# Half-block units of a mixture-of-experts kernel: tokens stationary, weights moving, in the first layer

## The chip, the cores and the metric

The kernel runs on one core of a Trainium2 chip. The metric is the device time of one execution in microseconds (us). Engines are named TensorE (PE in the profile; PEld are its weight loads), VectorE (DVE), ScalarE (ACT), GpSimd (POOL) and SyncE (SP, which issues most of the transfers).

## What is computed

A pooled attention makes 4608 rows of 512 numbers, and a mixture of eight experts is applied to them, each row going through the one expert that its gate picks:

```python
logits = x @ w_gate                      # x: 4608 x 512, the attention's output
expert_idx = np.argmax(logits, axis=1)
...
gate_w = probs[np.arange(N), expert_idx]
for e in range(E):                       # E = 8
    mask = expert_idx == e
    ...
    xe = x[mask]
    h = np.maximum(xe @ w1[e], 0.0)      # w1[e]: 512 x 1024
    ye = h @ w2[e]                       # w2[e]: 1024 x 512
    out[mask] = gate_w[mask, None] * ye
```

With the inputs that are timed here the experts get 1018, 55, 333, 239, 827, 724, 24 and 1388 rows.

## The kernel before

The first part (attention, gate, scattering the rows by expert) is not touched. The second part, in the function `experts`, works in **units**: up to 512 rows of one expert, counted in half blocks of 64 rows (n = 1 to 8). Here there are 13 units, numbered from 0, and their n is 8, 8, 1, 6, 4, 8, 5, 8, 4, 1, 8, 8, 6. The change concerns the units with n = 1, which are unit 2 (55 rows of expert 1) and unit 9 (24 rows of expert 6). The plan of the units is a table that every engine reads into registers, so each engine's program has branches by n.

Full precision is kept by splitting: every operand is a high part, rounded to the matmul's format, and a low part, the rest. W1H, W1L, W2H, W2L are the parts of an expert's two weight matrices in SBUF, XH and XL those of the rows (transposed, features by rows), HH and HL those of the hidden layer. For n = 1 the low parts of the 64 rows stand beside the high ones in 128 columns.

For a unit, the engines do this:

- TensorE (`form`): the first layer `mm1`, in eight slices of 128 hidden features (`f` = 0 to 7; L860 is its matmul, weights stationary, rows moving). A slice goes to one of three PSUM banks, pP0, pP1 and pq, in turn, so slice f waits until the low part of slice f - 3 is done (`V_h`), and it waits for the two parts of its piece of weights (`split`). Then, for n up to 2, the next unit's rows are transposed (`xt_all`, L813), and the second layer follows (`product`, L882), for n = 1 with 16 matmuls of 512 columns, two for each k of eight. The second layer's piece for k = 6 and 7 is the last that it waits for.
- ScalarE: for each slice the Relu that makes the high part (`hhi`, L968), and between them the casts of the unit's four second-layer pieces (`whi` 4 to 7, L1058); then the next unit's rows (`xhi`, L1031) and the casts of the next unit's four first-layer pieces (`whi` 0 to 3), all in program order.
- VectorE: for n up to 2 first the sum of the two halves of a slice in PSUM (`hsum`, L973), then the low part of the hidden slice (`hlo`, L989), and one low part of weights (`wlo`, L1066, piece 4). Then the next unit's rows (`xlo`, L1046), its pieces 0 and 2 (`wlo`), and the unit's own output (`y`, which for a half block is three operations, L1165, L1167 and L1169, by way of Y2), and then the next unit's slices.
- GpSimd: the previous unit's scatters of output rows (L1357), the low parts of pieces 5, 6 and 7 (L1066), then of the next unit's pieces 1 and 3.
- SyncE: in one queue the rows of a later unit (L1245), their gates (L1237), and the pieces of a later expert's weights into the staging tile ST (L1280). The second-layer pieces wait, where n is under 3, until the unit's second layer is done:

```python
                    if half:
                        with sp.If(entry(sp, K_U, u, 1, 8) < 3):
                            sp.wait_ge(Q["P_y"], 4 * u + 4)
                    for i in ii:
                        free(i)
                        stage_piece(i, e)
```

A wait of any engine holds what stands behind it in that engine's program. What the sums read and write before:

```python
dve.tensor_reduce(out=H1[g % 3], in_=pH[g % 3][:, : 2 * P].rearrange("p (a t) -> p t a", a=2), ...)   # PSUM to PSUM
src = H1[g % 3] if n <= 2 else pH[g % 3]
return dve.scalar_tensor_tensor(out=dst[:, f, to], in0=src[:, at], scalar=0.0, in1=f32(HH[:, f, at]), ...)
```

## Time and profile before

| | us |
|---|---|
| median of 3 runs | 624.31 (624.09 to 625.96) |
| profiled execution, its own time | 623.57 |
| its span in the profile | 621.9 |
| unit 2 on TensorE (its first matmul to unit 3's) | 263.47 to 277.19 |
| unit 9 on TensorE (its first matmul to unit 10's) | 476.67 to 491.33 |

The times in the profile count from the span's start. A row of a timeline has start, duration, engine, line, operation, what it writes from what it reads, shape and count, and in brackets the idle time ahead of it with what ended it. Rows of groups have the busy time and the mean duration of one in ns after the bar. In the chain of work that ended last, each row is a stretch of the path that sets the end.

### The profile page before, as it was taken

The numbers are of one execution on the slowest core, as the hardware profiler recorded it, in microseconds if no ns is written. First come the engines' busy times: TensorE is split into PE (matmuls) and PEld (weight loads), VectorE is DVE, ScalarE is ACT, GpSimd is POOL, SyncE is SP. The second block draws the span as 40 slices with busy tenths as digits, with TensorE's granted clock in tenths as the row PEclk, the third lists the DMA queues.
The fourth block names the chain that finished last, engine by engine and source line by source line (L and its number), as shares of the span: only waits on it lengthen the run. The fifth ranks groups of instructions, "written<-read, shape, count | busy, mean of one in ns | idle before, by whom it ended". The sixth has DMA issues, their size and how long they took to land.

```text
span 621.9 us, 13480 instructions
## 1 busy us (share of the span) xinstructions
PE 598.6 (96%) x4412; PEld 510.8 (82%) x4412; DVE 349.7 (56%) x731; ACT 240.5 (39%) x453; POOL 243.3 (39%) x288
## 2 busy tenths in 40 slices
PE   6989999999999999999999999999999999999995
PEld 5778989888877888899897889888898878888994
DVE  7699898888761325377576433854146764133220
ACT  2567776876511114075364311523034541021110
POOL 7457656655321222278545311251106861101101
PEclk9999999999999999999999999999999999999999
DMA  8999997981334671719578551074305360101001
GB/s 321 368 277 280 301 286 250 250 252 61 130 119 137 175 244 47 220 40 307 181 213 270 137 173 36 3 213 137 104 35 159 84 188 23 53 0 37 36 4 53
DMA packets 93937, 96.47 MB, mean 155 GB/s; under 512 B 43102, under 2 KB 74846, under 8 KB 93792
## 3 DMA queue, kind: packets, MB, share of 16 engines
q1 hardware_dynamic: 85808, 74.27, 41.0%
q0 software_dynamic: 7440, 20.50, 9.0%
q8 instruction: 60, 0.98, 0.6%
q14 instruction: 85, 0.70, 0.4%
q10 hardware_dynamic: 544, 0.02, 0.0%
HBM read 72.68 MB, written 26.00 MB: 159 GB/s over the span
## 4 chain that ended last, share of the span: by engine, by line
PE 72%; DVE 9%; issue 5%; POOL 4%; SPq 3%; ACT 3%; DMA 2%; POOLq 1%; DVEq 0%; ACTq 0%
PE pU L882 31%; PE pP L860 18%; PE pq L860 9%; PE pU L299 4%; DMA XE<-in_v_dram 2%; PE pP L283 2%; PE pP L463 2%; POOL dispatched L407 2%; PE pS L263 2%; SPq L1245 1%; PE pq L253 1%; ACT W L1058 1%; DVE mx L267 1%; DVE raw L172 1%; POOL raw L172 1%
## 5 line engine op out<-in xcount | busy, mean ns | idle before, releaser
L882 PE MATMUL pU<-W,H 128*128 128x512 f32 x912 | 216.4, 397 | 0.0
L882 PEld LDWEIGHTS pU<-W,H 128*128 128x128 f32 x912 | 171.3, 188 | 41.0
L860 PE MATMUL pP<-X,W 128*128 128x512 f32 (+3 forms) x748 | 143.2, 345 | 2.9 <-DVEq L1406 1.6
L860 PEld LDWEIGHTS pP<-X,W 128*128 128x128 f32 x748 | 122.8, 188 | 19.6 <-DVE H L989 2.3
L1357 POOL DMA_INDIRECT out_dram<-Y,GT x51 | 54.2, 1063 | 192.5 <-DVE Y L1171 169.4
L1066 POOL TENSOR_TENSOR W<-ST,W 128x1024 fp32r<-128x1024 f32 x30 | 77.7, 2605 | 84.1 <-ACT W L1058 84.0
L968 ACT ACTIVATE H<-pP 128x512 fp32r<-128x512 f32 (+1 forms) x67 | 36.0, 537 | 189.0 <-PE pP L860 153.2
L1171 DVE TENSOR_SCALAR Y<-pU,GT 128x512 f32<-128x512 f32 x36 | 27.0, 750 | 106.6 <-PE pU L882 105.6
L989 DVE SCALAR_TENSOR_TENSOR H<-pP,H 128x512 fp32r<-128x512 f32 (+2 forms) x73 | 42.2, 580 | 69.8 <-ACT H L968 68.0
L860 PE MATMUL pq<-X,W 128*128 128x512 f32 (+3 forms) x364 | 72.9, 348 | 0.9 <-DVE H L989 0.6
L860 PEld LDWEIGHTS pq<-X,W 128*128 128x128 f32 x364 | 60.1, 188 | 9.9 <-DVE H L989 1.1
L1058 ACT CAST W<-ST 128x1024 fp32r<-128x1024 f32 x56 | 57.1, 1056 | 7.6 <-DMA ST<-in_moe_w_dram 7.6
L299 PE MATMUL pU<-V,pt 110*128 110x146 f32 (+3 forms) x468 | 56.7, 283 | 1.3 <-ACT pt L284 0.8
L299 PEld LDWEIGHTS pU<-V,pt 110*128 110x128 f32 (+3 forms) x468 | 51.4, 179 | 3.0 <-ACT pt L284 1.8
L1066 DVE TENSOR_TENSOR W<-ST,W 128x1024 fp32r<-128x1024 f32 x26 | 42.7, 1645 | 7.5 <-ACT W L1058 7.4
L407 POOL DMA_INDIRECT dispatched<-xe,ix x36 | 39.8, 1107 | 18.2 <-POOL ix L368 9.8
L968 ACT ACTIVATE H<-pq 128x512 fp32r<-128x512 f32 (+1 forms) x33 | 17.9, 541 | 70.6 <-PE pq L860 69.1
L989 DVE SCALAR_TENSOR_TENSOR H<-pq,H 128x512 fp32r<-128x512 f32 (+2 forms) x35 | 20.8, 594 | 28.3 <-ACT H L968 27.5
L284 ACT COPY pt<-pP 110x384 f32<-110x384 f32 x72 | 30.9, 481 | 6.5 <-PE pP L283 5.8
L276 ACT ACTIVATE P<-sd 128x576 f32<-128x576 f32 x36 | 24.8, 689 | 19.6 <-DVE sd L270 17.7
L172 POOL TENSOR_TENSOR raw<-raw 128x768 f32<-128x768 f32 (+1 forms) x18 | 26.6, 1476 | 13.0 <-DMA raw<-in_v_dram 12.2
L1046 DVE TENSOR_TENSOR X<-pS,X 128x512 fp32r<-128x512 f32 x34 | 22.0, 687 | 16.9 <-ACT X L1031 11.3
(185 smaller groups left out, 624.6 us busy)
## 6 DMA issues: line engine op xcount, KB each, us to landing
ST<-in_moe_w_dram SPq DMA_DIRECT2D x56, 512.0 KB, 6.1
raw<-in_k_dram SPq DMA_DIRECT2D x12, 768.0 KB, 7.2
raw<-in_v_dram SPq DMA_DIRECT2D x11, 768.0 KB, 9.1
XE<-dispatched SPq DMA_DIRECT2D x104, 64.0 KB, 2.3
qa<-in_q_dram SPq DMA_DIRECT2D x24, 256.0 KB, 7.3
w<-in_moe_w_dram SPq DMA_DIRECT2D x8, 512.0 KB, 4.7
XE<-dispatched SPq DMA_DIRECT2D x15, 256.0 KB, 3.4
qa<-in_q_dram SPq DMA_DIRECT2D x2, 1024.0 KB, 11.3
```

The costliest lines, as they stand in the source:

```text
L172: return lambda: eng.tensor_tensor(out=out, in0=raw[:, :, 0:n], in1=raw[:, :, n : 2 * n], op=ALU.add)
L284: take(out=pt[t][a][0:R], in_=pPs[a][0:R, 0 : 3 * P])
L299: nc.tensor.matmul(pu[p0 : p0 + n, a, h * VW : (h + m) * VW], lhsT=pt[t][a][0:r, c % 3 * P + p0 : c % 3 * P + p0 + n], rhs=Vs[g % 2][0:r, ...
L407: apart(nc.gpsimd.indirect_dma_start(out=xs, out_offset=bass.IndirectOffsetOnAxis(ap=at, axis=0), in_=rows, in_offset=None))
L860: r = pe.matmul(out=pH[g % 3][:, :m], lhsT=w1s(w, f, k), rhs=x, start=i == 0, stop=i == len(passes) - 1)
L882: r = pe.matmul(out=pY[:, s % 2, :], lhsT=h, rhs=w[:, k * 512 : (k + 1) * 512], start=start and i == 0, stop=stop and i == len(ps) - 1, sk ...
L968: act.activation(out=HH[:, f, o], in_=src[:, o], func=AF.Relu).then_inc(Q["A_h"], 1)
L989: return dve.scalar_tensor_tensor(out=dst[:, f, to], in0=src[:, at], scalar=0.0, in1=f32(HH[:, f, at]), op0=ALU.max, op1=ALU.subtract)
L1058: act.copy(out=(W1H if i < 4 else W2H)[:, o], in_=ST[:, i, :]).then_inc(Q["A_s1" if i < 4 else "A_s2"], 1)
L1066: eng.tensor_tensor(out=(W1L if i < 4 else W2L)[:, o], in0=ST[:, i, :], in1=f32((W1H if i < 4 else W2H)[:, o]), op=ALU.subtract).then_inc( ...
L1171: r = dve.tensor_scalar(out=Y[:, s, :], in0=a, scalar1=gate, scalar2=None, op0=ALU.mult)
L1357: pool.indirect_dma_start(out=out, out_offset=bass.IndirectOffsetOnAxis(ap=GT[:, u, s, 1:2].bitcast(I32), axis=0), in_=Y[:, s, :], in_offs ...
```

## The change

For n = 1 the first layer is turned around. The 128 columns of the rows (64 high, 64 low) are the stationary operand, and the weights move, 512 columns at a time: two halves of the hidden layer (a = 0, 1), each with four blocks k of input features and two weight parts, 16 matmuls. The result has rows by partition, so ScalarE copies a half (128x512) to SBUF (`htake`, tile HR), TensorE transposes it in four pieces into another bank (`ht`), and VectorE adds the high rows' part and the low rows' part (`hsums`, tile HS, in SBUF). The Relu (`hhi1`) and the low part (`hlo1`) then work on 128x256, a half of the hidden layer, in place of eight slices of 128x64. The low parts of the rows are put beside the high ones in XH (`xnone`). The second half's transposes stand between the transposes of the next unit's rows, its Relu and low part behind the first block of the next unit's rows. Other units are as they are.

```diff
+    HR = sb.tile([P, 2, 512], F32, name="HR")
+    HS = sb.tile([P, 2, 256], F32, name="HS")
...
-        def xt_all(u):
+        def xt_all(u, mid=lambda: None):
             xt01(u)
+            mid()
...
+        halves_of = lambda w: w.rearrange("p (a i k f) -> p a k i f", a=2, i=2, k=4)
+        rows_h = [HR[:, a, :] for a in range(2)]
+        sums_h = [HS[:, a].rearrange("p (f t) -> p f t", f=4) for a in range(2)]
+        def hbank(u, a):
+            return pH[(8 * u + a) % 3]
+        def tbank(u, a):
+            return pH[(8 * u + (2, 0)[a]) % 3]
+        def mm1_rows(u, a, ks=range(4)):
+            if ks[0] == 0:
+                pe.wait_ge(Q["V_h"], 8 * u - 2 + a)
+                for i in range(2):
+                    split(pe, "s1", u, 2 * a + i)
+            for k in ks:
+                for w in (W1H, W1L):
+                    r = pe.matmul(out=hbank(u, a).rearrange("p (i f) -> p i f", i=2), lhsT=XH[:, k, 0:P], rhs=halves_of(w)[:, a, k],
+                                  start=k == 0 and w is W1H, stop=k == 3 and w is W1L, skip_group_check=True)
+            if ks[-1] == 3:
+                r.then_inc(Q["P_h"], 2)
+        def ht(u, a):
+            if a == 0:
+                pe.wait_ge(Q["V_h"], 8 * u)
+            pe.wait_ge(Q["A_h"], 8 * u + 2 + 2 * a)
+            for f in range(4):
+                r = pe.transpose(tbank(u, a)[:, f * P : (f + 1) * P], rows_h[a][:, f * P : (f + 1) * P], ident)
+            r.then_inc(Q["P_h"], 2)
...
-                mm1(u, n)
+                if n > 1:
+                    mm1(u, n)
+                else:
+                    mm1_rows(u, 0)
+                    mm1_rows(u, 1, range(2))
+                    ht(u, 0)
+                    mm1_rows(u, 1, range(2, 4))
...
-                more(pe, u + 1, lambda: xt_all(u + 1) if u else xt01(u + 1))
+                turned = (lambda: ht(u, 1)) if n == 1 and u > 0 else (lambda: None)
+                more(pe, u + 1, lambda: xt_all(u + 1, turned) if u else xt01(u + 1), turned)
...
+        def htake(u, a):
+            act.wait_ge(Q["P_h"], 8 * u + 2 + 4 * a)
+            act.copy(out=rows_h[a], in_=hbank(u, a)).then_inc(Q["A_h"], 2)
+        def hsums(u, a):
+            dve.wait_ge(Q["P_h"], 8 * u + 4 + 4 * a)
+            dve.tensor_reduce(out=sums_h[a], in_=tbank(u, a).rearrange("p (f a t) -> p f t a", f=4, a=2), axis=AX.X, op=ALU.add).then_inc(Q["V_1"], 4)
+        def hhi1(u, a):
+            act.wait_ge(Q["V_1"], 8 * u + 4 + 4 * a)
+            act.activation(out=HH[:, 4 * a : 4 * a + 4, 0:64], in_=sums_h[a], func=AF.Relu).then_inc(Q["A_h"], 2)
+        def hlo1(u, a):
+            dve.wait_ge(Q["A_h"], 8 * u + 6 + 2 * a)
+            dve.scalar_tensor_tensor(out=HH[:, 4 * a : 4 * a + 4, 64:128], in0=sums_h[a], scalar=0.0, in1=f32(HH[:, 4 * a : 4 * a + 4, 0:64]),
+                                     op0=ALU.max, op1=ALU.subtract).then_inc(Q["V_h"], 4)
...
+        def xnone(u, v):
+            if v < 2:
+                return vnop("V_x", v)
+            with dve.If(entry(dve, K_U, u, 1, 8) < 2):
+                dve.drain()
+                dve.tensor_tensor(out=XH[:, :, 64:P], in0=xbank(0, False).rearrange("p (k t) -> p k t", k=4)[:, :, 0:64], in1=f32(XH[:, :, 0:64]), op=ALU.subtract).then_inc(Q["V_x"], v)
...
-                    go(1)
+                    with act.If(entry(act, K_SW, u, 0, 1) == 1):
+                        whi(u, 4)
+                        whi(u, 5)
+                        htake(u, 0)
+                        whi(u, 6)
+                        whi(u, 7)
...
+                    htake(u, 1)
+                    hhi1(u, 0)
...
-                    go(1)
+                    with dve.If(entry(dve, K_SW, u, 0, 1) == 1):
+                        wlo(u, 4)
...
+                    hsums(u, 0)
+                    hlo1(u, 0)
+                    hsums(u, 1)
...
-        def xpart(eng, u, f, nop, mid=lambda: None, turn=None):
+        def xpart(eng, u, f, nop, mid=lambda: None, turn=None, first=lambda: None):
             f(u, 0, 1)
+            first()
             f(u, 1, 1)
...
+                        go(True, first=lambda: hhi1(u, 1))
...
+                        go(small=True, first=lambda: hlo1(u, 1))
```

The first `go(1)` is in ScalarE's `hidden_hi`, the second in VectorE's `hidden_lo`; `xpart` splits the next unit's rows on both.

The order on the engines shows it at the places that the prediction speaks of, all in unit 2's branch for n = 1. First TensorE, before (the last two of eight slices, then the next unit's rows; XE holds those, pS, pm and pU are PSUM):

```order
L860 MATMUL pP_66<-X,W 128x256 x8
L860 MATMUL pq<-X,W 128x256 x8
L813 MATMUL pS<-ident,XE_3050 128x128 x8
L839 COMPARE_AND_BRANCH
L840 COMPARE_AND_BRANCH
L813 MATMUL pm<-ident,XE_3050 128x128 x4
```

And TensorE in the changed program, from the unit's start:

```order
L885 MATMUL pP_66<-W,X 128x512 x8
L885 MATMUL pq<-W,X 128x512 x4
L896 MATMUL pP_65<-ident,HR 128x128 x4
L885 MATMUL pq<-W,X 128x512 x4
L815 MATMUL pS<-ident,XE_3050 128x128 x8
L896 MATMUL pP_66<-ident,HR 128x128 x4
L842 COMPARE_AND_BRANCH
L843 COMPARE_AND_BRANCH
L815 MATMUL pm<-ident,XE_3050 128x128 x4
```

Eight slices of eight matmuls have become sixteen matmuls, with the first half's transposes among the second half's products and the second half's behind two blocks of the next unit's rows.

VectorE before, at the end of the unit (sum of one slice, low parts, then the next unit's rows):

```order
L973 TENSOR_REDUCE pq<-pq 128x128
L989 SCALAR_TENSOR_TENSOR H<-pP_66,H 128x64
L989 SCALAR_TENSOR_TENSOR H<-pq,H 128x64
L1115 UNCONDITIONAL_BRANCH
L1179 COMPARE_AND_BRANCH
L1121 COMPARE_AND_BRANCH
L1046 TENSOR_TENSOR X<-pS,X 128x4x128 x2
```

And VectorE in the changed program, the unit's hidden layer:

```order
L1137 TENSOR_TENSOR W<-ST,W 128x1024
L1197 UNCONDITIONAL_BRANCH
L796 COPY scr<-scr 128x1
L1199 UNCONDITIONAL_BRANCH
L1013 TENSOR_REDUCE HS<-pP_65 128x256
L1021 SCALAR_TENSOR_TENSOR H<-HS,H 128x4x64
L1013 TENSOR_REDUCE HS<-pP_66 128x256
```

The sixteen small operations are four, of which two read HS and H in place of a PSUM bank; the second low part follows the first block of the next unit's rows:

```order
L1107 TENSOR_TENSOR X<-pS,X 128x4x128
L1021 SCALAR_TENSOR_TENSOR H<-HS,H 128x4x64
L1107 TENSOR_TENSOR X<-pS,X 128x4x128
L1081 COMPARE_AND_BRANCH
L1107 TENSOR_TENSOR X<-pm,X 128x4x128
```

Here the low part has moved in between the next unit's first and second block.

More of the change, by code (lines that the diff above doesn't have):

```diff
@@ L1046, in xlo @@
             dve.tensor_tensor(out=XL[:, :, o], in0=xbank(s, spare).rearrange("p (k t) -> p k t", k=4), in1=f32(XH[:, :, o]), op=ALU.subtract).then_inc(Q["V_x"], inc)
+        def xnone(u, v):
[4 more added lines that the diff above has]
+                dve.tensor_tensor(out=XH[:, :, 64:P], in0=xbank(0, False).rearrange("p (k t) -> p k t", k=4)[:, :, 0:64], in1=f32(XH[:, :, 0:64]), op=ALU.subtract).then_inc(Q["V_x"], v)
+            with dve.Else():
+                vnop("V_x", v)
         def split(eng, n, u, i):
@@ L1092, in hidden_hi @@
                 with act.Else():
-                    go(1)
+                    with act.If(entry(act, K_SW, u, 0, 1) == 1):
[4 more added lines that the diff above has]
+                        whi(u, 7)
+                    with act.Else():
+                        anop("A_s2", 4)
+                        htake(u, 0)
+                    htake(u, 1)
+                    hhi1(u, 0)
         def hidden_lo(u, fs=range(8), small=True):
@@ L1115, in hidden_lo, with next_part @@
                 with dve.Else():
-                    go(1)
-        def next_part(eng, u, xf, xnop, wf, wnop, turn=None, mid=lambda: None, between=2):
+                    with dve.If(entry(dve, K_SW, u, 0, 1) == 1):
+                        wlo(u, 4)
+                    with dve.Else():
+                        vnop("V_s2", 2)
+                    hsums(u, 0)
+                    hlo1(u, 0)
+                    hsums(u, 1)
+        def next_part(eng, u, xf, xnop, wf, wnop, turn=None, mid=lambda: None, between=2, first=lambda: None):
             sw = entry(eng, K_SW, u, 0, 1)
             with eng.If(sw == 0):
-                xpart(eng, u, xf, xnop, mid, turn)
+                xpart(eng, u, xf, xnop, mid, turn, first)
                 wnop()
@@ L1125, in next_part @@
                 ii = range(4) if eng is act else (0, 2)
-                xpart(eng, u, xf, xnop, lambda: [mid(), *(wf(u, i) for i in ii if i < between)], turn)
+                xpart(eng, u, xf, xnop, lambda: [mid(), *(wf(u, i) for i in ii if i < between)], turn, first)
                 for i in ii:
@@ L1139, in following, with go @@
             def following():
-                def go(small):
-                    next_part(act, u + 1, lambda *a: xhi(*a, small), lambda v: anop("A_x", v), whi, lambda: anop("A_s1", 4), between=0 if small else 2)
+                def go(small, **first):
+                    next_part(act, u + 1, lambda *a: xhi(*a, small), lambda v: anop("A_x", v), whi, lambda: anop("A_s1", 4), between=0 if small else 2, **first)
                 if u == 0:
@@ L1147, in following, with alone @@
                 with act.Else():
-                    go(True)
+                    with act.If(entry(act, K_U, u, 1, 8) > 1):
+                        go(True)
+                    with act.Else():
+                        go(True, first=lambda: hhi1(u, 1))
+            def alone():
+                if u > 0:
+                    with act.If(entry(act, K_U, u, 1, 8) < 2):
+                        hhi1(u, 1)
             if u > 0:
                 hidden_hi(u)
-            more(act, u + 1, following)
+            more(act, u + 1, following, alone)
             if u + 2 < NU:
@@ L1174, in following @@
             def following():
-                go = lambda turn=None, small=False, **mid: next_part(dve, u + 1, lambda *a: xlo(*a, small), lambda v: vnop("V_x", v), wlo, lambda: vnop("V_s1", 2), turn,
+                go = lambda turn=None, small=False, **mid: next_part(dve, u + 1, lambda *a: xlo(*a, small), lambda v: xnone(u + 1, v), wlo, lambda: vnop("V_s1", 2), turn,
                                                                      between=0 if small else 2, **mid)
@@ L1181, in following, with alone @@
                 with dve.Else():
-                    go(small=True)
+                    with dve.If(n > 1):
+                        go(small=True)
+                    with dve.Else():
+                        go(small=True, first=lambda: hlo1(u, 1))
                     early()
+            def alone():
+                if u > 0:
+                    with dve.If(n < 2):
+                        hlo1(u, 1)
+                early()
             def early():
@@ L1205, in dve_unit @@
                 hidden_lo(u)
-            more(dve, u + 1, following, early)
+            more(dve, u + 1, following, alone)
             if u + 2 < NU:
```

## The prediction

> **What bounds the kernel now.** I read the page's busy shares first, then TensorE's timeline, then the chain of work that ended last around the units that the change touches, then the timelines of VectorE, GpSimd, ScalarE and the DMA queue there.
>
> ```profile
> PE 598.6 (96%) x4412; PEld 510.8 (82%) x4412; DVE 349.7 (56%) x731; ACT 240.5 (39%) x453; POOL 243.3 (39%) x288
> ```
>
> TensorE is busy for 96% of the span, so time on it counts, unless it then stands waiting. Which units have one half block is read from the widths of L860's matmuls and the counts of L882's. Two units have 64 matmuls of 256 columns (8 a slice) and then 16 of L882: unit 2, from 263.47, and unit 9, from 476.67 (counted from 0). Unit 2 on TensorE (start, duration, engine, line, count):
>
> ```profile
> 240.97 22.65 PE L882 MATMUL pU<-W,H 128*128 128x512 f32 x96
> 263.47 1.12 PE L860 MATMUL pP<-X,W 128*128 128x256 f32 x8
> 264.43 1.12 PE L860 MATMUL pq<-X,W 128*128 128x256 f32 x8
> ...
> 272.01 1.14 PE L813 MATMUL pS<-ident,XE 128*128 128x128 f32 x8
> ...
> 273.38 3.98 PE L882 MATMUL pU<-W,H 128*128 128x512 f32 x16
> 277.19 4.40 PE L860 MATMUL pP<-X,W 128*128 128x384 f32 x24
> ```
>
> A matmul of 512 columns takes 0.234 us there (96 from 240.97 to 263.47), one of 256 columns 0.12 us (8 in 0.96). Unit 3 begins at 277.19, and its fourth slice stands still until VectorE is ready, as the chain shows:
>
> ```profile
> 280.59 0.69 DVE Y L1165
> ...
> 283.70 0.61 DVE H L989
> 284.31 0.04 issue
> 284.36 4.50 PE pP L860 x24
> ```
>
> So what counts at the first place is not when TensorE ends unit 2, but when VectorE has done unit 2's output (three operations from 280.59) and unit 3's first slice. VectorE in turn waits here for GpSimd:
>
> ```profile
> 264.63 0.43 DVE L973 TENSOR_REDUCE pP<-pP 128x128 f32<-128x256 f32 x1 [0.21 <-PE pP L860]
> 265.21 0.98 POOL L1357 DMA_INDIRECT out_dram<-Y,GT  x1 [4.65 <-DVE Y L1171]
> 267.44 7.14 POOL L1066 TENSOR_TENSOR W<-ST,W 128x1024 fp32r<-128x1024 f32 x3 [1.25 <-ACT W L1058]
> 269.67 0.22 DVE L989 SCALAR_TENSOR_TENSOR H<-pP,H 128x64 fp32r<-128x64 f32 x1
> 273.64 1.29 DVE L1046 TENSOR_TENSOR X<-pS,X 128x512 fp32r<-128x512 f32 x2 [0.49 <-ACT X L1031]
> 275.66 1.23 DVE L1066 TENSOR_TENSOR W<-ST,W 128x1024 fp32r<-128x1024 f32 x1
> 276.65 5.88 POOL L1066 TENSOR_TENSOR W<-ST,W 128x1024 fp32r<-128x1024 f32 x2 [2.06 <-ACT W L1058]
> 277.55 2.70 DVE L1066 TENSOR_TENSOR W<-ST,W 128x1024 fp32r<-128x1024 f32 x1 [0.67 <-ACT W L1058]
> 281.38 1.44 DVE L1167 TENSOR_SCALAR Y<-Y,GT 64x512 f32<-64x512 f32 x1
> 401.29 0.48 DVE L1167 TENSOR_SCALAR Y<-Y,GT 64x512 f32<-64x512 f32 x1
> ```
>
> GpSimd's split of a piece takes 7.14 / 3 = 2.38 us. VectorE's takes 1.23 alone (275.66) and 2.70 beside GpSimd (277.55). Taken as a queue for one door this fits: GpSimd's first split ends at 276.65 + 2.39 = 279.04, VectorE's then needs 1.21, which is 280.25, its recorded end; GpSimd's second ends at 282.53, some 2.3 later. VectorE's scaling of Y2 behaves alike (1.44 beside GpSimd, done 0.29 after its end at 282.53; 0.48 without). But VectorE operations with an input in PSUM, in the middle of GpSimd's three splits (269.67, 273.64), take what they always take. So: **a VectorE operation that reads only SBUF waits for the GpSimd split that is running, and the next split waits for it; one that reads PSUM does not.**
>
> **The change, part by part.** Removed on TensorE, a unit: 64 x 0.12 = 7.68 us. Added: 16 x 0.234 = 3.75 for the turned products, and 8 transposes at 0.121 (8 of L813 from 272.01 to 272.98) = 0.97. Net 2.96 us less work a unit, 5.9 in all. What lies behind it decides how much of that is left.
>
> The new steps' durations, from the nearest rows:
>
> ```profile
> L255 ACT COPY qT<-pq 128x512 f32<-128x512 f32 x36 | 21.2, 589 | 11.5 <-PE pq L253 11.3
> L968 ACT ACTIVATE H<-pq 128x512 fp32r<-128x512 f32 x28 | 16.8, 599 | 69.1 <-PE pq L860 69.1
> 272.67 0.22 ACT L968 ACTIVATE H<-pq 128x64 fp32r<-128x64 f32 x1 [0.74 <-DVE pq L973]
> 273.02 1.07 ACT L1031 CAST X<-pS 128x512 fp32r<-128x512 f32 x2
> 274.55 3.91 ACT L1058 CAST W<-ST 128x1024 fp32r<-128x1024 f32 x4
> L267 DVE TENSOR_REDUCE mx<-pS 128x8 f32<-128x576 f32 x36 | 27.1, 752 | 4.4 <-PE pS L263 4.4
> L989 DVE SCALAR_TENSOR_TENSOR H<-pq,H 128x512 fp32r<-128x512 f32 x28 | 19.3, 688 | 27.6 <-ACT H L968 27.3
> ```
>
> The copy of a half out of PSUM is L255's form, 0.59 (0.5 apart in a row of them). The Relu of 256 columns lies between 0.22 (64) and 0.60 (512): 0.38. The sum over 512 elements lies between 0.43 (256) and 0.75 (576): 0.70. The low part of 256 columns lies between 0.22 and 0.69 by width: 0.42; but both its inputs, HS and HH, are now in SBUF, where before one was PSUM. No row shows this operation beside a split. Its lower bound is 0.42 (it passes, as L989 does), its upper 0.42 plus what is left of a split, up to 2.38 (it queues, as L1066 and L1167 do). I take the upper: both operations seen that read SBUF alone queue, and what set L989 apart, its PSUM input, is gone.
>
> *Unit 2, on the profile's clock.* ScalarE may start when TensorE ends unit 1 (240.97 + 22.65 = 263.62): four casts at 0.955, two copies between them at 0.5, the first Relu 0.38, ends 263.66 + 3.82 + 1.0 + 0.38 = 268.86. TensorE keeps ahead of the copies (products done at 267.9). GpSimd is free after its scatter at 266.19 and its casts are there, so its splits run 266.19, 268.57, 270.95. The first low part asks at 268.9, 0.3 us after the second split began, and waits until 270.95: done 271.4. The third split moves to 271.4-273.75. Behind the low part on VectorE stands the sum of the second half (0.70, done 272.05); its Relu is done at 272.45, and the second low part waits for the third split: 273.75-274.2. L882's first eight matmuls run meanwhile, from 271.4; the last eight end near 276.1, against 277.36 now: TensorE is 1.3 us early.
>
> Behind that stands the next unit. ScalarE's second X cast starts at 272.45 instead of 273.5 (the second of the two from 273.02), so GpSimd's first split for unit 3, which now comes 3.15 after that, could start at 275.6. VectorE's second X operation starts after the low part, at 274.15; now 1.4 lie from there (274.26) to its split at 275.66, so it asks at 275.5. VectorE comes first by 0.1 (up to 0.2, since each handover in the rows overlaps by about 0.1). Then split, GpSimd's split, split, and unit 2's output follow as now, 0.1 to 0.5 us earlier. The fourth slice starts so much earlier than 284.36: **0.3 us gained, of 2.96**. Before VectorE's sums and Relus went slice by slice under the matmuls; now the last of them are bare, but those waits are inside this sum. ScalarE's copies (4 x 0.5 in both units) replace small Relus and lie inside it too.
>
> The transfers of unit 3's second-layer pieces wait for the end of unit 2 on TensorE, so they come 1.3 early, no limit. What xnone adds (one VectorE operation, 128x256 from PSUM, under 0.69, in units 1 and 8) is hidden by L882 there (22.65 us in unit 1; 48 matmuls, 11 us by 0.234 each, in unit 8): without that cover 0.4 each.
>
> *Unit 9.* Here GpSimd first issues four scatters, then splits, and TensorE's gain is spent in unit 10 (first the timelines of GpSimd, the DMA queue and TensorE, then the chain):
>
> ```profile
> 481.65 7.17 POOL L1066 TENSOR_TENSOR W<-ST,W 128x1024 fp32r<-128x1024 f32 x3
> 480.01 10.14 SPq L1245 DMA_DIRECT2D XE<-dispatched  x16
> 490.78 2.78 SPq L1237 DMA_DIRECT2D GT<-dispatched  x4
> 491.33 3.03 PE L860 MATMUL pq<-X,W 128*128 128x512 f32 x12 [0.23 <-issue]
> 496.17 3.70 DMA ST<-in_moe_w_dram
> 499.89 1.06 ACT W L1058
> 500.97 1.23 DVE W L1066
> 502.20 0.61 DVE H L989
> 502.86 5.86 PE pP L860 x24
> ```
>
> The splits start at 481.65 whatever TensorE does. Reckoned as above, the low parts go between them at 484.0 and 486.8, the third ends near 489.5, and unit 10 starts near 490.5 instead of 491.33. But its fifth slice (502.86) waits for a chain that starts with a transfer at 496.17. SyncE issues that one after the x rows (until 490.15) and gates (until 493.56) in a row. Its wait for the end of unit 9 (273.38 + 3.98 is the like in unit 2; here about 491) is over by then, so TensorE's being early doesn't move it. So 0.8 are early and 0.8 are waited: **0**.
>
> **Sum:** -0.3 + 0 = -0.3 us. The profiled execution took 623.57 (span 621.9 and 1.67 around it), so 623.3; the median of the runs is 624.31, 0.74 above, and 0.3 off that is **624.0 us**. A change under about 0.3% (1.9 us) can't be told from none.
>
> [...]
>
> **The rivals.**
>
> *The low parts pass.* If this operation is like L989 as it was, they take 0.42 each. The second sum ends at 270.15, the X casts and ScalarE's casts for unit 3 run 2.6 us earlier than 274.55, and with them VectorE's output and the fourth slice: -2.6, so 621.7. For it: no row shows the new form beside a split. Against it: two forms that queue. 0.22.
>
> *The first low part slips in.* If it asks before 268.57 (0.3 earlier than I reckon), or GpSimd starts 0.3 later, one split's wait is saved, and unit 3's fourth slice moves by 1.9: 622.4. 0.07.
>
> *GpSimd takes the door first (the other side).* At the start of unit 3 both ask within 0.1 us. If VectorE's ask comes more than 0.1 later than reckoned, GpSimd's split runs first, VectorE's first split ends at 279.2 instead of 276.9, its second at about 282.5, and the output and the fourth slice slip 1.0 to 1.5: 625.5. For it: today's margin of 0.99 (275.66 against 276.65) is used up. Against it: the handovers' overlap. 0.20.
>
> *All of TensorE's saving counts*, 5.9: 618.4. Against it stand both waits above. 0.02.
>
> **How the numbers follow.** The forecast has 0.44 and its own range is 623.5 to 624.6; 0.05 is for what I don't see. The range reaches from the first rival with a little (621.6) to GpSimd first at its dearer end with 0.3 for branches (625.8). Faster by over 0.3% (under 622.4): the first rival, half of the slip, and the whole saving, 0.27. Slower by over 0.3% (over 626.2): GpSimd first with a second loss of 1.1 at unit 10 or a dearer handover, and half of the unseen, 0.10. Within: 0.63.
>
> **What the profile after would show.** Right: 16 turned matmuls in 3.9 us; the low part on 128x256 lasting 2 us and more in unit 2 while GpSimd's splits run; VectorE's first split for unit 3 ahead of GpSimd's; the fourth slice of unit 3 starting about 20.6 us after the unit 2 products began (20.9 now); the fifth slice of unit 10 behind the same transfer. Wrong: low parts at 0.42 beside GpSimd (then 621.7), or a turned matmul dearer than 0.234, which the copies' slack of 0.1 would pass on.

## The result, and the profile after

The changed kernel takes 633.22 us (median of 4 runs, 629.41 to 636.54) against 625.02 before (4 runs, 624.09 to 625.96): a ratio of 1.0137, 95% interval 1.0098 to 1.0177. It is slower by 1.4%, outside the forecast's range. Its own runs lie in two pairs, near 629.7 and 636.5; the profiled one took 636.54, with a span of 634.9. The granted clock by slices (tenths of full speed, 40 slices of the span) has two dips, where the two half-block units are:

```profile
PEclk9999999999999999979999999999999799999999
```

By windows, from a half-block unit's first matmul to the next unit's (length, then busy time and count of PE, PEld, DVE, ACT, POOL, then the granted clock, DMA share and GB/s), first the changed kernel's units 2 and 9, then the same of before:

```profile
263.48:281.83 18.35, 13.33 (x54) 10.11 (x53) 14.61 (x12) 10.97 (x16) 12.15 (x6) 0.81 0.10 26
485.54:504.48 18.94, 13.40 (x58) 10.43 (x56) 15.36 (x13) 11.42 (x16) 13.20 (x8) 0.82 0.58 159
```

```profile
263.47:277.19 13.72, 13.11 (x93) 12.18 (x92) 9.52 (x23) 9.60 (x19) 8.66 (x5) 1.00 0.12 33
476.67:491.33 14.66, 13.79 (x97) 12.53 (x96) 9.99 (x23) 10.15 (x19) 11.93 (x8) 1.00 0.56 148
```

Unit 2 is 4.63 us longer and unit 9 4.28, with fewer matmuls on TensorE. Its busy time did not fall by the 2.96 us that were taken off: the granted clock was 0.81 instead of 1.00 in unit 2, and 0.82 in unit 9. VectorE's busy time rose by 5 us in each; an instruction that waits once it has started counts as busy (5.20 us below for 0.43 of work). Unit 2 in the timelines of TensorE, GpSimd and VectorE after the change:

```profile
263.48 2.03 PE L885 MATMUL pP<-W,X 128*128 128x512 f32 x8
...
274.29 1.65 PE L918 MATMUL pU<-W,H 128*128 128x512 f32 x4 [4.03 <-DVE H L1021]
276.72 5.27 PE L918 MATMUL pU<-W,H 128*128 128x512 f32 x12 [0.79 <-DVE H L1021]
281.83 4.40 PE L863 MATMUL pP<-X,W 128*128 128x384 f32 x24
...
265.22 1.68 POOL L1461 DMA_INDIRECT out_dram<-Y,GT  x1 [4.65 <-DVE Y L1266]
266.93 7.02 POOL L1137 TENSOR_TENSOR W<-ST,W 128x1024 fp32r<-128x1024 f32 x3
278.37 5.86 POOL L1137 TENSOR_TENSOR W<-ST,W 128x1024 fp32r<-128x1024 f32 x2 [4.42 <-ACT W L1129]
...
269.03 5.20 DVE L1021 SCALAR_TENSOR_TENSOR H<-HS,H 128x256 fp32r<-128x256 f32 x1 [1.24 <-ACT H L1017]
275.46 0.43 DVE L1021 SCALAR_TENSOR_TENSOR H<-HS,H 128x256 fp32r<-128x256 f32 x1
277.38 1.23 DVE L1137 TENSOR_TENSOR W<-ST,W 128x1024 fp32r<-128x1024 f32 x1 [0.17 <-ACT W L1129]
```

The first low part (L1021) starts, that is asks, at 269.03 and is done at 274.23. It is 0.43 of work, as the second shows. In between lies not the rest of one split of GpSimd but the rest of all three, to 273.95, in one piece straight behind the scatter's issue (265.22 + 1.68 = 266.90). TensorE stands 4.03 for it. The 12 matmuls behind take 5.27, 0.44 each, where 0.234 was the measure before. Unit 9 does the same, and unit 3 has a third such place:

```profile
489.27 0.98 POOL L1461 DMA_INDIRECT out_dram<-Y,GT  x1 [0.30 <-issue]
490.25 6.99 POOL L1137 TENSOR_TENSOR W<-ST,W 128x1024 fp32r<-128x1024 f32 x3
491.09 6.43 DVE L1021 SCALAR_TENSOR_TENSOR H<-HS,H 128x256 fp32r<-128x256 f32 x1 [1.24 <-ACT H L1017]
497.58 2.08 PE L918 MATMUL pU<-W,H 128*128 128x512 f32 x4 [5.18 <-DVE H L1021]
...
289.77 0.98 POOL L1461 DMA_INDIRECT out_dram<-Y,GT  x1 [0.30 <-issue]
290.77 4.77 POOL L1137 TENSOR_TENSOR W<-ST,W 128x1024 fp32r<-128x1024 f32 x2
290.48 6.15 DVE L1137 TENSOR_TENSOR W<-ST,W 128x1024 fp32r<-128x1024 f32 x1 [0.46 <-ACT W L1129]
...
297.28 6.04 PE L863 MATMUL pP<-X,W 128*128 128x384 f32 x24 [2.57 <-DVE H L1049]
```

There VectorE's split asked while the scatter was still being issued (289.77 to 290.75) and waited for both splits behind it. It came that late because unit 3's pieces are sent only after unit 2's end, which was 4.6 late; the chain leads back to that transfer:

```profile
283.66 5.71 DMA ST<-in_moe_w_dram
...
289.40 1.06 ACT W L1129
```

Unit 3 lost 3.46. With 0.76 in unit 4 and -0.41 in unit 10 the sum is 12.7 of the 13.0 us between the two profiled spans.

### The profile page after: what moved, and what is told of

Read it like the earlier page. It is cut to its first block, busy times and chain, and to the rows that moved or that the text cites. A ratio compares the mean times of both kernels' runs of the same rounds, so it can differ in the third digit from the quotient of the medians.

```text
span 634.9 us, 13314 instructions
## 1 busy us (share of the span) xinstructions
PE 599.7 (94%) x4332; PEld 508.3 (80%) x4332; DVE 368.1 (58%) x707; ACT 241.1 (38%) x445; POOL 241.0 (38%) x288
## 4 chain that ended last, share of the span: by engine, by line
PE 73%; DVE 9%; issue 5%; DMA 4%; POOL 3%; ACT 3%; SPq 2%; DVEq 0%; ACTq 0%; POOLq 0%
PE pU L918 35%; PE pP L863 18%; PE pq L863 9%; PE pU L299 3%; DVE H L1021 2%; DMA XE<-in_v_dram 2%; PE pP L463 2%; POOL dispatched L407 2%; PE pP L283 2%; ACT W L1129 2%; PE pS L263 1%; DVE mx L267 1%; SPq L228 1%; DVE sd L270 1%; PE pq L253 1%
## 5 line engine op out<-in xcount | busy, mean ns | idle before, releaser
L918 PE MATMUL pU<-W,H 128*128 128x512 f32 x912 | 222.0, 404 | 10.3 <-DVE H L1021 10.0
L863 PE MATMUL pP<-X,W 128*128 128x512 f32 (+3 forms) x660 | 132.8, 356 | 4.7 <-DVE H L1049 2.6
L863 PEld LDWEIGHTS pP<-X,W 128*128 128x128 f32 x660 | 113.3, 190 | 20.9 <-DVE H L1049 2.9
L1028 ACT ACTIVATE H<-pP 128x512 fp32r<-128x512 f32 x56 | 33.5, 598 | 172.6 <-PE pP L863 165.7
L1049 DVE SCALAR_TENSOR_TENSOR H<-pP,H 128x512 fp32r<-128x512 f32 (+1 forms) x62 | 39.8, 644 | 73.8 <-ACT H L1028 72.0
L863 PE MATMUL pq<-X,W 128*128 128x512 f32 (+3 forms) x324 | 67.1, 356 | 0.1
L1137 DVE TENSOR_TENSOR W<-ST,W 128x1024 fp32r<-128x1024 f32 x26 | 54.0, 2076 | 6.2 <-ACT W L1129 6.2
L1028 ACT ACTIVATE H<-pq 128x512 fp32r<-128x512 f32 x28 | 16.7, 598 | 71.8 <-PE pq L863 71.8
L1049 DVE SCALAR_TENSOR_TENSOR H<-pq,H 128x512 fp32r<-128x512 f32 (+1 forms) x30 | 19.7, 657 | 26.8 <-ACT H L1028 25.9
L172 POOL TENSOR_TENSOR raw<-raw 128x768 f32<-128x768 f32 (+1 forms) x18 | 26.9, 1493 | 12.7 <-DMA raw<-in_v_dram 12.0
L283 PE MATMUL pP<-ident,P 128*110 128x128 f32 x216 | 30.0, 275 | 0.6 <-ACT P L276 0.6
```

The costliest lines, as they stand in the source:

```text
L172: return lambda: eng.tensor_tensor(out=out, in0=raw[:, :, 0:n], in1=raw[:, :, n : 2 * n], op=ALU.add)
L283: nc.tensor.transpose(pPs[a][0:R, c * P : (c + 1) * P], Ps[t % 2][:, o : o + R], ident)
L863: r = pe.matmul(out=pH[g % 3][:, :m], lhsT=w1s(w, f, k), rhs=x, start=i == 0, stop=i == len(passes) - 1)
L918: r = pe.matmul(out=pY[:, s % 2, :], lhsT=h, rhs=w[:, k * 512 : (k + 1) * 512], start=start and i == 0, stop=stop and i == len(ps) - 1, sk ...
L1028: act.activation(out=HH[:, f, o], in_=src[:, o], func=AF.Relu).then_inc(Q["A_h"], 1)
L1137: eng.tensor_tensor(out=(W1L if i < 4 else W2L)[:, o], in0=ST[:, i, :], in1=f32((W1H if i < 4 else W2H)[:, o]), op=ALU.subtract).then_inc( ...
```

## Experiments

The kernels of one comparison share a chip, and what runs ahead takes differently long from trace to trace (unit 2 begins between 263.21 us, in e10, and 274.23, in e7; the kernel before had medians of 632.2, 631.4, 623.6 and 632.6 us in the four comparisons), so kernels are compared by their ratio to the kernel before on the same chip and by the length of unit 2 in their own profile. The kernel before has one trace, the first; the changed kernel itself was run in the first comparison and beside e1 to e4 alone.

| kernel | ratio to before, 95% interval | unit 2, us |
|---|---|---|
| before (first profile) | 1 | 13.72 |
| changed (first profile) | 1.0137 (1.0098 to 1.0177) | 18.35 |
| e1 sums in PSUM | 1.0078 (1.0051 to 1.0106) | 16.42 |
| e2 before, sums in SBUF | 1.0109 (1.0085 to 1.0133) | 19.38 |
| e3 changed, TensorE kept busy | 1.0059 (1.0033 to 1.0084) | 16.98 |
| e4 changed, again | 1.0078 (1.0054 to 1.0101) | 17.97 |
| e6 GpSimd waits for the low part | 1.0015 (0.9991 to 1.0039) | 14.24 |
| e7 VectorE splits | 1.0008 (0.9977 to 1.0039) | 14.05 |
| e8 e7 and sums in PSUM | 0.9989 (0.9957 to 1.0022) | 13.33 |
| e10 GpSimd starts behind a wait | 1.0089 (1.0049 to 1.0130) | 16.38 |
| e11 GpSimd stops between splits | 1.0012 (0.9996 to 1.0029) | 13.42 |
| e12 e11 and sums in PSUM | 0.9996 (0.9974 to 1.0018) | 12.41 |

**e1, the sums in PSUM.**

```diff
-        sums_h = [HS[:, a].rearrange("p (f t) -> p f t", f=4) for a in range(2)]
+        sums_h = lambda u, a: hbank(u, 0)[:, 256 * a : 256 * a + 256].rearrange("p (f t) -> p f t", f=4)
```

> The changed kernel with one thing different: the sums of the turned halves go to a PSUM bank instead of the SBUF tile HS, so the two low parts of a half-block unit again have one input in PSUM. Theory P (the port: a VectorE operation that reads only SBUF waits until GpSimd's queued splits are all through, and TensorE waits for it): the low parts take about 0.43 us each instead of 5.20 and 6.43, and the time falls to 621 to 623 us, under the kernel before. Theory C (the longer chain of copy, transpose, sum, Relu and low part costs the time by itself, the port has little part in it): still 628 us or more.

```profile
271.47 11.79 POOL L1137 TENSOR_TENSOR W<-ST,W 128x1024 fp32r<-128x1024 f32 x5
273.63 0.42 DVE L1021 SCALAR_TENSOR_TENSOR H<-pP,H 128x256 fp32r<-128x256 f32 x1 [1.20 <-ACT H L1017]
277.27 8.21 DVE L1137 TENSOR_TENSOR W<-ST,W 128x1024 fp32r<-128x1024 f32 x2
284.49 6.96 PE L863 MATMUL pP<-X,W 128*128 128x384 f32 x24 [3.97 <-DVE W L1137]
```

With one input in PSUM the low part takes 0.42 in the middle of GpSimd's splits: the two SBUF inputs are what made it wait. But the time stayed lost, against theory P's 621 to 623 us. VectorE's splits for unit 3 now ask 9.2 us into the unit (277.27), 3.0 sooner than in the kernel before, while GpSimd is still in its chain. They wait for all five splits, the fourth of which was not even cast when they asked. The wait moved from one instruction to the next.

**e2, the kernel before with its sums in SBUF.** The other half of the question: the old order of work, with only the operand's place changed.

```diff
-    H1 = [b[:, 2 * P : 3 * P] for b in pH]
+    HT = sb.tile([P, 3, P], F32, name="HT")
+    H1 = [HT[:, i, :] for i in range(3)]
```

> The kernel before with one thing different: for units of one or two half blocks the sums of a slice go to SBUF instead of back to PSUM; the first layer is not turned. Theory P: the low parts that fall into GpSimd's three splits (267.44 to 274.58 in unit 2, 481.65 to 488.82 in unit 9) wait for the end of all three, TensorE's slices behind them wait too, and each of the two units gets 3 to 6 us longer: 630 to 637 us. Theory C: nothing is turned, so the time stays at 624 us within 0.3%.

```profile
276.89 4.73 POOL L1067 TENSOR_TENSOR W<-ST,W 128x1024 fp32r<-128x1024 f32 x2 [1.72 <-ACT W L1059]
277.38 1.98 DVE L990 SCALAR_TENSOR_TENSOR H<-HT,H 128x64 fp32r<-128x64 f32 x1
279.62 2.08 DVE L990 SCALAR_TENSOR_TENSOR H<-HT,H 128x64 fp32r<-128x64 f32 x1
```

0.22 became 1.63 to 2.09 us, six times in the two units, and the kernel about as slow as the changed one. But here VectorE waits for one split and is let in between two (277.38 + 1.98 = 279.36, just after the first split's end), not for all three as theory P had it. One split or all of them: that is the question for the next runs.

**e3, TensorE kept busy.** 20 bf16 matmuls of 512 columns (0.22 us each), whose result nothing uses, where it waits for the low part.

```diff
+                if n == 1 and u > 0:
+                    for _ in range(20):
+                        pe.matmul(out=hbank(u, 1)..., lhsT=ones, rhs=ones..., start=True, stop=True, ...)
```

> The changed kernel with 20 matmuls of 512 columns (bf16 ones, result unused, about 0.22 us each, 4.4 us in all) put where TensorE waits for the first low part in the two half-block units. It sizes what the granted clock adds: in the changed kernel 12 second-layer matmuls behind the wait take 5.27 us instead of about 2.9. If the lowered clock behind the wait is a cost of its own, these matmuls go back to 0.234 us each and the time falls by 2 to 5 us against the changed kernel. If not, it stays within 1 us of it. Theory P and theory C agree that the wait itself stays.

```profile
273.80 5.30 DVE L1024 SCALAR_TENSOR_TENSOR H<-HS,H 128x256 fp32r<-128x256 f32 x1 [1.24 <-ACT H L1020]
281.67 3.04 PE L918 MATMUL pU<-W,H 128*128 128x512 f32 x12 [1.32 <-DVE H L1024]
```

The 12 matmuls are back at 3.04 and the clock at 0.999, the wait is unchanged. Unit 2 is 1.0 us shorter than in e4. The ratio is 0.0019 lower (1.2 us), less than the 2 to 5 us expected, and the two intervals overlap. So in the trace the clock is a second loss that follows from the wait; the run times do not show its size.

**e4, the changed kernel once more**, on the same chip.

> The changed kernel again, for a second profile: its runs fell at about 629.5 and at about 636.5 us. Theory P: the low parts wait 5 to 6.5 us in both half-block units in each; between the two levels differs whether unit 3's later VectorE split (6.15 us from 290.48 in the first profile, 1.21 before) meets GpSimd's splits too, and TensorE behind it. Theory C: the low parts' duration does not tell the levels apart and neither does that split's.

The low parts again took 5.20 and 5.54. Unit 3's split did not meet the chain this time: its transfer landed later, GpSimd's second split was not cast yet, and VectorE waited for one split:

```profile
297.71 3.00 DVE L1137 TENSOR_TENSOR W<-ST,W 128x1024 fp32r<-128x1024 f32 x1 [0.91 <-issue]
```

Unit 3 took 34.25 here, 38.19 in the first profile and 34.73 before. So that loss comes and goes; units 2 and 9 (4.25 and 4.66 here) always pay. These 3.9 us may be the better part of the 6.8 between the changed kernel's two pairs of runs; the faster pair has no trace.

**e5, the door by itself.** A program with nothing but queued splits on GpSimd and one VectorE operation.

```python
for m in range(n):                       # n splits queued behind a running one
    if m == 0:
        pool.wait_ge(S["P2"], i + 1)     # released early, or at a set time
    r = pool.tensor_tensor(out=T["GC" + str(m + 1)], in0=T["GA"], in1=T["GB"], op=ALU.subtract)
```

> A program of its own: nothing of the reference is computed (zeros are stored). GpSimd makes one 128x1024 subtraction out of SBUF (the split), with 0, 1, 2 or 4 more queued behind it, whose release comes either at the start or at a set time within the first; VectorE asks some 0.6 us into the first split, with the low part's operation (128x256, both inputs in SBUF), with a 128x1024 subtraction, with the low part's operation that has one input in PSUM, with a reduction out of PSUM, or with a multiplication by a column. Theory K (GpSimd keeps the door for every split that is ready when the one in front ends): with 1, 2 and 4 ready behind, the low part lasts to the end of the last one, 4, 6.5 and 11 us; where the next split's release comes less than about 1 us before the end of the running one, VectorE is let in after the first, 1.5 to 2.2 us. Theory F (first come, first served, the one of the prediction): VectorE waits for the running split alone in every trial, 1.5 to 2.2 us, and the next split waits for it. Both: an input in PSUM, the reduction and the column's multiplication run at their 0.2 to 0.8 us at once.

```profile
193.46 2.34 POOL L112 TENSOR_TENSOR GC<-GA,GB 128x1024 f32<-128x1024 f32 x1 [0.98 <-ACT SB L104]
195.76 9.41 POOL L116 TENSOR_TENSOR GC<-GA,GB 128x1024 f32<-128x1024 f32 x4
193.84 2.24 DVE L125 SCALAR_TENSOR_TENSOR VC<-VA,VB 128x256 f32<-128x256 f32 x1 [5.85 <-ACT SB L106]
169.93 0.42 DVE L127 SCALAR_TENSOR_TENSOR VC<-PB,VB 128x256 f32<-128x256 f32 x1 [3.56 <-ACT SB L106]
```

With four ready splits in the queue VectorE is let in after the running one (2.24), in every trial (1.48 to 2.42 for the low part, 2.28 to 3.22 for the wide subtraction), whatever the release. Theory K, that GpSimd keeps the door for each ready split, falls; the prediction's queue holds here. A miss beside it: the multiplication by a column, which both theories let pass, took 2.24 as well (the prediction had read it so: 1.44 instead of 0.48).

**e6, GpSimd waits for the first low part** before its second split.

```diff
                         with pool.If(entry(pool, K_U, u, 1, 8) < 3):
+                            pool.wait_ge(Q["V_h"], 8 * u + 4)
                             wlo(u, 6, True)
```

> The changed kernel with one wait more: GpSimd starts its second split of the second layer only when the first low part is done. Theory K (the door is kept for every ready split): the first low part of unit 2 waits for the end of the one split that runs and lasts under 1.3 us instead of 5.20; the two splits held back then run together, and the second low part, asked some 2 us later, waits for both and lasts 3 to 4.5 us, so that unit 2 gains 1 us or less of its 4.6. Theory F (first come, first served): the first low part is as in K, but the second waits for one split at most, under 2.4 us, and unit 2 gains 2 us or more.

```profile
274.18 11.69 POOL L1137 TENSOR_TENSOR W<-ST,W 128x1024 fp32r<-128x1024 f32 x4 [0.37 <-DVE H L1021]
275.44 1.43 DVE L1021 SCALAR_TENSOR_TENSOR H<-HS,H 128x256 fp32r<-128x256 f32 x1
```

The second low part is let in behind the first of four splits, the next one ready: first come, first served once more, and K falls in the kernel too. Unit 2 gains 4.1 us. What the two kinds of chain differ in: every chain of several splits that kept VectorE out stands straight behind a scatter's issue (266.93, 490.25 and 290.77 in the changed kernel, 271.47 in e1), every one that let it in began behind a wait for a semaphore.

**e7 and e8, no GpSimd split in the unit.** VectorE makes pieces 4 to 7 of a half-block unit, and GpSimd leaves out its three; e8 has e1's sums in PSUM as well.

```diff
                         wlo(u, 4)
+                        wlo(u, 5, own=True)
+                        hsums(u, 0)
+                        wlo(u, 6, own=True)
+                        hlo1(u, 0)
+                        hsums(u, 1)
+                        wlo(u, 7, own=True)
```

> The changed kernel with the sums in SBUF as they are, but in half block units VectorE makes all four splits of the second layer (1.23 us each), two ahead of the first sum, one between it and the first low part, one behind the second sum; GpSimd makes none there. Theory K (the loss is the door that GpSimd's queued splits keep): both low parts of units 2 and 9 take 0.42 to 0.45 us, TensorE's wait for them shrinks from 4.03 to under 1.5 us, unit 2 takes 11 to 13 us from its first matmul to the next unit's (18.35 in the changed kernel, 13.72 before), and the kernel is 0.2 to 0.8% faster than before. Rival C (the chain product, copy, turn, sum, high part, low part is itself too long): the wait ahead of the second layer stays 2.5 us or more with low parts of 0.43 us, and unit 2 stays above 14 us, the ratio at 1.003 or more.

> As the kernel with VectorE's four splits, and the sums stay in PSUM, so that the low parts read one input in SBUF only. Theory K: no GpSimd split is left in the half block unit that a low part could meet, so PSUM or SBUF for the sums makes no difference: both kernels within 0.3% of each other. Rival C (chain): the same low parts, and unit 2 above 14 us. If the low parts of the other kernel still meet GpSimd's splits of the next unit's first layer, this one is faster by those waits, 0.5 to 2.4 us a unit.

In e7:

```profile
283.86 4.59 PE L918 MATMUL pU<-W,H 128*128 128x512 f32 x12 [1.89 <-DVE H L1021]
284.12 4.57 DVE L1137 TENSOR_TENSOR W<-ST,W 128x1024 fp32r<-128x1024 f32 x2
```

All low parts take 0.41 to 0.43 in both, and the loss against before is gone, so GpSimd's splits in the unit were what cost it. The gain that was expected of e7 did not come, and neither side was wholly right: the wait ahead of the second layer is 1.89 (under 1.5 by theory K, 2.5 or more by rival C), unit 2 takes 14.05 (11 to 13, above 14). VectorE's own four splits stand ahead of the second low part, the clock falls in e7 (12 matmuls in 4.59; 3.05 in e8 after the same 1.89), and VectorE's next two splits still meet GpSimd's (4.57 for two). The two kernels can't be told apart.

**e9, what stands in front of the chain.** As e5, with different things ahead of three or five splits.

```python
if a == "put":
    pool.indirect_dma_start(out=out, out_offset=bass.IndirectOffsetOnAxis(ap=IDX, axis=0), in_=Z, ...)
elif a == "stall":
    pool.wait_ge(S["P2"], stalls)
elif a == "copy":
    pool.tensor_copy(out=T["GD"][:, 0:1], in_=T["GA"][:, 0:1])
```

> A program of its own again (zeros are stored, the reference is not computed): chains of three or five ready GpSimd splits, with VectorE asking within the first, second or last of them, and in each trial something else in front of the chain on GpSimd: a wait for a semaphore, an indirect DMA's issue, that issue and a drain, that issue and a wait, that issue and a small copy or a memset, a copy alone, that issue with a wait behind the first split. Theory D (a chain that follows an indirect DMA's issue without a wait in between holds the door to its end): with the issue straight ahead, VectorE's low part ends with the last split, 4 to 7 us after it asks (9 or more with five splits), and with a wait for a semaphore between issue and chain, or no issue at all, it is let in after the running split, 0.5 to 2.4 us. Theory T (what decides is when in the split VectorE asks): asking late in a split or in a later one keeps it out with and without an issue ahead. Theory F alone: 2.4 us or less in all trials.

The issue straight ahead, then the issue and a drain, then the issue and a wait:

```profile
39.19 1.12 POOL L114 DMA_INDIRECT out_dram<-Z,IDX  x1 [1.76 <-ACT SB L98]
39.87 7.69 DVE L138 SCALAR_TENSOR_TENSOR VC<-VA,VB 128x256 f32<-128x256 f32 x1 [6.94 <-ACT SB L100]
40.34 6.93 POOL L110 TENSOR_TENSOR GC<-GA,GB 128x1024 f32<-128x1024 f32 x3
...
83.41 0.99 POOL L114 DMA_INDIRECT out_dram<-Z,IDX  x1 [2.01 <-ACT SB L98]
84.19 0.42 DVE L138 SCALAR_TENSOR_TENSOR VC<-VA,VB 128x256 f32<-128x256 f32 x1 [2.50 <-ACT SB L100]
...
95.13 0.99 POOL L114 DMA_INDIRECT out_dram<-Z,IDX  x1 [1.67 <-ACT SB L98]
96.20 7.11 POOL L110 TENSOR_TENSOR GC<-GA,GB 128x1024 f32<-128x1024 f32 x3
96.65 2.16 DVE L138 SCALAR_TENSOR_TENSOR VC<-VA,VB 128x256 f32<-128x256 f32 x1 [12.04 <-ACT SB L100]
```

| ahead of the chain | low part, us (two trials) |
|---|---|
| a wait | 2.24, 2.30; 2.25, 2.25 |
| a small copy, no issue | 2.20, 2.18 |
| the issue, three splits | 7.69, 7.46 |
| the issue, five splits | 12.06, 12.05 |
| the issue, asked 1.6 us into the first split | 5.61, 5.62 |
| the issue, asked at the second split's start | 4.87, 4.86 |
| the issue and a small copy | 7.60, 7.61 |
| the issue and a memset | 7.44, 7.43 |
| the issue and a wait | 2.16, 2.16 |

(The row "asked at the second split's start" is a trial with a wait behind the first split, which was fulfilled before it was reached and made no stop. In the last row the wait did stop the queue, if only just: 0.08 us lie between issue and chain, 0.02 or 0.03 where nothing stands between.) Each low part behind an issue that no stop of the queue follows ends with the chain's last split: theory D, and T falls, since VectorE is kept out wherever it asks. The wide subtraction behaves alike (8.26 with three splits, 12.84 with five, 3.10 behind a wait). In one more trial the low part came before the issue and shows nothing. In the one with a drain behind the issue, which held GpSimd's queue for 2.1 us, it asked 0.78 us into the issue and took 0.42. So the issue alone does not keep VectorE out. Straight ahead of a chain it does: there an ask 0.68 us into the issue waited for the whole chain (39.87).

**e10, the chain behind a wait, in the kernel.**

```diff
+                    if ii[0] > 4:
+                        with pool.If(entry(pool, K_U, u, 1, 8) < 2):
+                            pool.wait_ge(Q["A_h"], 8 * u + 4)
                     wlo(u, ii[0])
```

> The changed kernel; in half block units GpSimd waits, ahead of its three splits of the second layer, until ScalarE has copied the second half of the products, so that the chain of splits begins behind a wait instead of straight behind the indirect DMA's issue (in unit 2 it starts 1.7 us later than in the changed kernel, in unit 9 0.3 to 0.5 us). The three splits are all ready then, as before. Theory D: the first low part waits for the running split alone, under 2.6 us instead of 5.20 and 6.43, the second too, and units 2 and 9 lose 1.5 to 3.5 us of their 18.35 and 18.94. Theory K (every ready split keeps the door): the first low part waits for all three, 5.5 to 7 us, and unit 2 gets longer than 18.35.

```profile
268.60 14.21 POOL L1137 TENSOR_TENSOR W<-ST,W 128x1024 fp32r<-128x1024 f32 x5 [1.97 <-ACT HR L1009]
268.76 2.52 DVE L1021 SCALAR_TENSOR_TENSOR H<-HS,H 128x256 fp32r<-128x256 f32 x1 [1.24 <-ACT H L1017]
272.50 1.31 DVE L1021 SCALAR_TENSOR_TENSOR H<-HS,H 128x256 fp32r<-128x256 f32 x1
274.73 5.02 PE L918 MATMUL pU<-W,H 128*128 128x512 f32 x12 [2.09 <-DVE H L1021]
```

The same splits start later, and VectorE gets in after one, twice. Unit 2 is 1.97 shorter than in the changed kernel, unit 9 3.14. The clock stays low (0.988 over the span, where before it is 0.998; the 12 matmuls take 5.02). The ratio does not show the gain: its interval overlaps e4's, and the profiled run is the fastest of its six (627.08 to 633.25).

**e11 and e12, a stop between two splits.** GpSimd waits for its own split before; e12 has the sums in PSUM as well.

```diff
+                            pool.wait_ge(Q["G_s2"], 2 * (u - 1) + 1)
                             wlo(u, 6, True)
+                            pool.wait_ge(Q["V_s2"], 2 * (u - 1) + 2)
                     wlo(u, ii[1])
```

> The changed kernel; in half block units each of GpSimd's second and third split first waits for GpSimd's own split in front of it, so that its queue stands still for a moment between two splits; nothing waits for VectorE. Theory D (a chain behind an indirect DMA's issue holds the door only while it runs through): VectorE is let in at the first of these stops, the first low part of unit 2 lasts under 1.3 us and the second under 2.8, and unit 2 takes 13.5 to 15.5 us. Theory H (the issue holds the door until something other than GpSimd's own end releases it): the low part waits for all three splits and two stops, 5.3 to 6.5 us, and unit 2 takes 18 us or more.

> The same two waits, and the sums stay in PSUM, so that the low parts have one input in SBUF only. Theory D: the low parts take 0.42 us; VectorE's splits of the next unit, which waited 8.21 us for two through the chain of five in the kernel with the sums in PSUM alone, are let in one by one, each within 2.4 us of asking plus its 1.23; unit 2 takes 12.3 to 14 us (13.72 before) and the kernel is 0.3% faster to 0.3% slower than before. Theory H: as with the sums in PSUM alone, 8 us for the two splits and unit 2 above 16 us, ratio 1.006 to 1.01.

```profile
274.05 4.95 POOL L1137 TENSOR_TENSOR W<-ST,W 128x1024 fp32r<-128x1024 f32 x2
279.25 9.14 POOL L1137 TENSOR_TENSOR W<-ST,W 128x1024 fp32r<-128x1024 f32 x3 [0.25 <-POOL W L1137]
276.15 0.59 DVE L1021 SCALAR_TENSOR_TENSOR H<-HS,H 128x256 fp32r<-128x256 f32 x1 [1.24 <-ACT H L1017]
278.08 1.20 DVE L1021 SCALAR_TENSOR_TENSOR H<-HS,H 128x256 fp32r<-128x256 f32 x1
280.20 3.04 PE L918 MATMUL pU<-W,H 128*128 128x512 f32 x12 [1.89 <-DVE H L1021]
```

These lines are e11's. A short stop is enough: the first low part is let in at the one between the first two splits (0.08 us of standing in the trace), the second at the next (0.25). The low parts take 0.59 and 1.20, unit 2 13.42, and the kernel is level with before, 4 us better by ratio than e4 (on another chip): theory D. In e12 unit 2 is 12.41, 1.3 shorter than before, VectorE's two splits take 5.30 instead of 8.21, and the time is still the same as before within its interval. Units 2 and 3 together gain 2.1 us, unit 9 nothing, and unit 10 takes 27.2 us up to its second layer (22.8 before): its fifth slice stands 2.88 for a low part behind a piece of weights that landed late. No version here beats the kernel before. In e11's unit 2 TensorE has 2.57 us less to do than before, but it stands for 2.88 where it stood for 0.61: 1.89 of them ahead of the last 12 matmuls, 0.77 ahead of unit 3. Of the 1.89, 0.92 come after the second low part is done (279.28 to 280.20; the same in e6, e7, e8 and e10), where in the changed kernel the first four started 0.06 after theirs. What fills them the traces don't show.

## Why the prediction was wrong

- **TensorE's 2.96 us less work** was nearly right: the 16 turned matmuls fill 3.91 us (263.48 to 267.77, less 0.38 for the four transposes between them), and in e11, where the clock is 1.00 in unit 2, TensorE is busy 10.54 us there instead of 13.11, 2.57 less.
- **When the low part asks** was right: reckoned 268.9, measured 269.03. So was the new steps' cost (Relu 0.42, sum 0.69, low part 0.43).
- **How long it waits** is the step that failed. "The next split waits for it" was read from rows 276.65 and 277.55, where GpSimd's chain began behind a wait (2.06 for ScalarE). The prediction itself put GpSimd's first split right at the scatter's end, and so knew that in the new kernel that wait would be gone: before, the casts came between the Relus and GpSimd stood 1.25 us between scatter and splits. It did not see that such a wait is what lets VectorE in (2.16 us with it and 7.69 without in e9, 2.52 in e10). A wait of 2.05 us was reckoned (268.9 to 270.95), 4.77 came (5.20 less 0.43 of work). By the prediction's own queue it would have been 0.3: GpSimd's chain began at 266.93, 0.74 later than reckoned (the scatter's issue took 1.68, not 0.98, with a split of VectorE beside it this time), so the low part asked inside the first split, which ended at 269.34. That is the condition of the rival in which the low part slips in; it came true, and the low part waited for all three all the same. In the trace of before no VectorE operation with two SBUF inputs ran beside a chain of several splits straight behind a scatter, so the longer wait could not be read there. What could be read was that the price came from chains that had begun in another way.
- **The second layer's first eight matmuls** were to run while the second low part waited. Four ran (274.29); the other 12 waited for it (276.72), though it took no more than 0.43 here. So even with the waits as reckoned TensorE would have ended four matmuls, 0.9 us, later than 276.1.
- **The clock** was left out. The wait cost TensorE its full clock: 12 matmuls in 5.27 (granted clock 0.52 from 276.70 to 281.83) instead of 2.8 to 3.04; kept busy in e3, it took 3.04. In the changed kernel the 12 came after 4.03 us of standing, four matmuls and 0.79 more. Shorter waits had slow matmuls behind them too: 1.34 and 2.09 us with four matmuls between them gave 5.02 in e10, and 1.89 gave 4.59 in e7 but 3.04 in e11. What decides between 4.59 and 3.04 no run here shows.
- **Unit 9's zero** was wrong, since the unit ended not early but 4.28 late, and unit 10 gave back only 0.41. An early end did not pay either, as forecast, and cost more than reckoned: in e7 unit 9 is 1.27 shorter than before and unit 10 3.27 longer, its fifth slice standing 3.24 for a low part. In none of e6, e7, e8, e10, e11 and e12 are units 9 and 10 together shorter than before (0.1 to 4.4 us longer, one trace each).
- **VectorE's split ahead of GpSimd's at unit 3** was right (277.38 and 278.37), so the rival on the other side, GpSimd first, did not happen there. A loss that no rival had came later in unit 3: at 290.48 a chain behind a scatter kept VectorE out, and the unit lost 3.46.
- **That two SBUF inputs set the new low part apart** was right: beside GpSimd's splits it takes 0.42 with one input in SBUF (e1) and 5.20 with two, and in e2 two made 1.63 to 2.09 us out of 0.22. A multiplication by a column waits as well, 2.24 us in e5. Behind an indirect DMA's issue the measured hold is a whole chain, 7.02 us in unit 2 and 11.79 in e1.

## What to carry to other kernels

Where two engines keep each other out, price a wait from a row whose neighbour began in the same way: GpSimd's queue behind a wait let VectorE in after one instruction (2.24 us in e9), behind an indirect DMA's issue only when it stopped (7.69 without a stop). Keep GpSimd's long SBUF work from running on out of an indirect DMA without a stop, or put in a short wait for its own last instruction (0.25 us or less here; unit 2 4.9 us shorter). And removing a wait can close a gap that another engine lived on.

## What the runs showed of the hardware

- Splits that GpSimd runs straight behind an indirect DMA's issue keep out a VectorE operation with two SBUF inputs until GpSimd's queue stands still: 7.69 us with three splits and 12.06 with five, against 2.24 beside three splits behind a wait (e9). Small operations in between (a copy 7.60, a memset 7.44) don't let it in; a wait that stops the queue does (2.16, and 0.59 in e11), a wait already fulfilled doesn't (4.87). Why, the traces don't show.
- VectorE's multiplication by a column, 128x512 with one tensor and a column out of SBUF, waits for GpSimd's split too (2.24 us in e5, as long as the two-input form in the same place).
- Kept busy by 20 bf16 matmuls (4.48 us) during the wait (e3; 4.03 us of standing in the changed kernel), TensorE ran the last 12 matmuls in 3.04 instead of 5.27 (4.88 in e4, on e3's chip).
